# Clustered attention and two MLP layers on one core: another order of a head pair's cycle

## The chip, the cores and the metric

The kernel runs on one core of a Trainium2 chip. Its engines take their instructions in program order, each from a queue of its own, and wait for each other by semaphores: TensorE (PE, with its weight loads as PEld), VectorE (DVE), ScalarE (ACT), GpSimd (POOL) and SyncE (SP), which issues nearly all DMAs here. The metric is the time of one execution on the device in microseconds, as the median of several runs.

## The reference

Attention with 2 batches, 8 heads, 768 positions and head dimension 64, in which a query sees only the keys of its own cluster (16 centroids per head), and then two MLP layers over 1536 tokens (512 to 2048 and back). All values are float32.

```python
q_assign = np.argmax(np.einsum('bhsd,hcd->bhsc', q_n, c_n), axis=-1)
k_assign = np.argmax(np.einsum('bhsd,hcd->bhsc', k_n, c_n), axis=-1)
mask = q_assign[:, :, :, None] == k_assign[:, :, None, :]
scores = scale * np.matmul(q, k.transpose(0, 1, 3, 2))
scores = np.where(mask, scores, -1000000000.0)
scores = scores - np.max(scores, axis=-1, keepdims=True)
attn = np.exp(scores)
attn = attn / (np.sum(attn, axis=-1, keepdims=True) + 1e-09)
x = np.matmul(attn, v)          # then heads side by side: 1536 x 512
...
h = x @ w_in;  x = (h * np.cos(h)) @ w_out          # first layer
h = x @ w_in;  x = g(h) @ w_out                     # second: 0, (h+1)^2/4 or h
```

## The kernel before, in words

The 16 heads (2 batches of 8) are worked off as 8 pairs of heads, one pair in each cycle, and while a pair's scores are made, the pairs after it are prepared and the pair before it is finished. The order is written out by hand, as strings of short words: BEGIN for cycle 0, CYCLE for cycles 1 to 5, LATE for 6, LAST for 7, then END. `run_cycle` (line 719) emits the instructions word by word, and each engine keeps that order in its own queue; only END is mixed with the first instructions of the MLP stage when the program is built. A word with an apostrophe belongs to the pair before; the words of preparation (Q, D, C, m, t, n, O, H, J) are for the pair two ahead, or with the apostrophe for the next pair. The words:

- Q0 to Q3 (`turn`): PE transposes a quarter of q and k of a pair, ACT copies it out (t32, L497), POOL splits it in a high and a low part (tt, L499 and L500).
- D, C, m, t, n: dot products with the centroids, transposed back, and the first largest found (PE L510, L518; DVE L527, L528, L537, L538; POOL L533). O: PE transposes the one-hot rows, ACT writes them to the tile oht (L547), of which there is one.
- H0, H1 (`stack`): five DMAs on SP's queue each, which send the split parts of head 0 or 1 to the stacked operands st of the scores (L473, st from tt). J0, J1: four small DMAs each, which send the one-hot rows there (st from oht). There are three buffers of each st for the four that two pairs need.
- S0 to S11: the scores of 128 queries of the pair (S0 to S5 head 0, S6 to S11 head 1; PE L583 and L586), and DVE's row maximum (nm, L593). The scores have two buffers. E0 to E11: ACT's exponential with the row sum (p, L601).
- Head 0: G0 to G11 transposes p (PE L644, ACT copy L646), V0 to V5 multiplies it by v (L651), X scales the result by the reciprocals (DVE L656, in the tile rb), Y splits x for the MLP (POOL L663 to L667).
- Head 1: T6 to T11 transposes p in strips on DVE (L677), W0 to W3 are 192 small strip products on PE (L686), Z adds their halves (ACT L696, DVE L697), z scales and splits (POOL L705 to L707).
- R0, R1 (`inverse`): the reciprocals of the row sums, put in a line by POOL (L614) and sent to DRAM (flat, L617). B0, B1 (`spread`): SP loads them back to many partitions (rb, L630 for head 0, L625 for head 1). For head 0 there is one buffer rb, which holds the reciprocals, then x: the next load of it waits until Y has read it.
- L, v, r: SP loads the next q and k, v, and v in strips (L235, L243, L254). w: one of six steps in the conversion of a chunk of MLP weights (SP L147, ACT L157, DVE L159 to L167 and L176, POOL L173).

SP issues in order, so what stands behind a waiting load waits with it. The tile `big`, four banks of PSUM, takes the results of Q, D, C, O, G, V and W. On every engine a writer of `big` waits for the reader that stood before it in the program, of whatever bank. After the cycles comes the MLP stage: three matmuls (L858 to L860) for each product, with float32 values in two parts, over four quarters of the hidden width and three blocks of tokens in each layer.

```python
def x_rows(i):
    x = rb[2 * i]
    nc.vector.tensor_tensor(x, big[:, 3, :HS], x, ALU.mult)
...
    rb[d] = xpool.tile([P, HS], F32, tag="rb", bufs=1, name=f"rb{d}")
```

Of the kernel before, what the change touches and what calls it, by code (L numbers as in the profile page):

```python
# [33 lines left out]
def attention_moe_moe(  # L34
# [19 lines left out]
    B, H, S, D = q.shape  # L54
    C = centroids.shape[1]
# [152 lines left out]
    with ExitStack() as actx:  # L208
# [510 lines left out]
        def run_cycle(c, order):  # L719
# [4 lines left out]
            for word in words:  # L724
# [62 lines left out]
                elif what == "w":  # L787
                    pump(arg or 1)

        BEGIN = ("L' S3 m' S4 E3 t' E4 S5 H0' n' E5 R0 G0 G1 G2 S6 G3 G4 E6 G5 O' J0' r S7 T6 E7 G6 G7 V0 H1' "  # L790
                 "B0 V1 S8 T7 E8 Q0 G8 G9 J1' G10 S9 V2 Q1 T8 E9 Q2 Q3 L S10 D E10 T9 G11 C m V3 t n S11 O")
        CYCLE = ("Q0 Q1 S0 E11' V4' T10' E0 Q2 S1 Q3 S2 E1 V5' X' T11' E2 D v' S3 G0 S4 E3 W0' W1' S5 E4 J0' W2' "
                 "R1' E5 W3' Z' S6 S7 L G1 G2 G3 E6 G4 r E7 C m V0 V1 G5 t G6 T6 B1' R0 n G7 S8 T7 G8 G9 z' G10 "
                 "S9 V2 E8 B0 O T8 E9 S10 E10 Y' J1' H1' V3 H0' G11 T9 S11")
        LATE = ("S0 E11' V4' T10' E0 S1 w S2 E1 V5' X' T11' E2 v' S3 G0 S4 E3 W0' W1' S5 w E4 J0' W2' "
                "R1' E5 W3' w Z' S6 S7 G1 G2 G3 E6 G4 r E7 w V0 V1 G5 G6 T6 B1' R0 G7 S8 T7 G8 G9 z' G10 "
                "S9 V2 E8 B0 T8 w E9 S10 E10 Y' J1' H1' V3 H0' G11 T9 w S11")
        LAST = ("S0 E11' V4' T10' E0 S1 w S2 E1 V5' X' T11' E2 v' S3 G0 S4 E3 W0' W1' S5 w E4 W2' "
                "R1' E5 W3' w Z' S6 S7 G1 G2 G3 E6 G4 r E7 w V0 V1 G5 G6 T6 B1' R0 G7 S8 T7 G8 G9 z' G10 "
                "S9 V2 E8 B0 T8 w E9 S10 E10 Y' V3 G11 T9 w S11")  # L800
        END = "E11' V4' T10' V5' T11' R1' X' W0' W1' B1' W2' W3' Z' Y' z'"
        first_pair()
        for c in range(NP):
            run_cycle(c, {0: BEGIN, 6: LATE, 7: LAST}.get(c, CYCLE))
        run_cycle(NP, END)
        manual.close()
# [7 lines left out]
    while len(wslot) < 2:  # L814
        n = len(wslot)
# [148 lines left out]
```

## Time and profile before

| | us |
|---|---|
| runs, median (lowest to highest of 3) | 990.74 (990.56 to 995.32) |
| the profiled execution, its own time | 992.61 |
| its span, first to last instruction | 990.8 |
| PE busy | 836.3 (84%) |
| DVE, ACT, POOL busy | 583.7, 365.1, 253.2 |

The span falls in two parts: the attention stage up to about 474 us, in which PE's granted clock changes between half and full speed and no engine is full, and the MLP stage after it, in which PE is busy throughout at full clock. In the rows below, a line of the time line gives the start, the duration, the engine and line, the operation with its tiles, how many instructions were merged, and in brackets how long the engine had been idle before and what ended that. A line of the waits gives the total, the number and the longest. In rows of SP, SPq, the duration is the time of issuing, not that of the transfer.

### The profile page before, as it was taken

The page shows a single profiled execution, that of the slowest core. Times are in us where ns is not written, and L with a number is a line of the kernel's source. Part 1 is how long each engine was busy: PE and PEld are TensorE (multiplying, and loading weights), DVE is VectorE, ACT ScalarE, POOL GpSimd, SP SyncE. Part 2 cuts the span into 40 slices and gives each one's busy share as a digit, 9 for nine tenths or more (in the row PEclk, how much of TensorE's full clock was granted, in tenths as well). Part 3 has the DMA queues.
Part 4 walks back from the last instruction along what each step waited for, and adds up shares of the span by engine and source line. Part 5 has one row for each costly group of instructions (what it writes and reads, how often), then busy time and mean ns, then how long its engine had stood idle before and what let it go on. Part 6 is the DMA issues. An engine that isn't in the chain of part 4 may idle for free.

```text
span 990.8 us, 12697 instructions
## 1 busy us (share of the span) xinstructions
PE 836.3 (84%) x4957; PEld 632.5 (64%) x4957; DVE 583.7 (59%) x805; ACT 365.1 (37%) x650; POOL 253.2 (26%) x374
## 2 busy tenths in 40 slices
PE   7668776776757583676899999999999999999998
PEld 3435453444435351445788888888888888888887
DVE  4434433344434353554877787788888778884553
ACT  4425343433434342342544343444322443322220
POOL 5022424242423122042412212122332212211110
PEclk9578676766858676768899999999999999999999
DMA  7251423435343423313122221222112212200012
GB/s 186 59 123 44 94 69 94 98 75 117 74 108 96 108 53 97 73 30 118 69 85 85 74 87 52 86 86 85 43 43 85 67 62 85 86 1 1 0 43 85
DMA packets 52620, 74.97 MB, mean 76 GB/s; under 512 B 28976, under 2 KB 36368, under 8 KB 52560
## 3 DMA queue, kind: packets, MB, share of 16 engines
q1 hardware_dynamic: 52272, 73.99, 27.0%
q8 instruction: 39, 0.64, 0.3%
q14 instruction: 21, 0.17, 0.1%
q10 hardware_dynamic: 288, 0.16, 0.1%
HBM read 50.89 MB, written 3.19 MB: 55 GB/s over the span
## 4 chain that ended last, share of the span: by engine, by line
PE 52%; DVE 0%; ACT 0%; issue 0%; DVEq 0%
PE y L859 9%; PE y L860 9%; PE y L858 9%; PE h L858 8%; PE h L859 8%; PE h L860 8%; ACT r L833 0%; DVE xs L697 0%; DVE g L837 0%; DVE r L832 0%; ACT r L834 0%; PE y_end L860 0%; PE y_end L859 0%; PE y_end L858 0%; DVE acc L910 0%
## 5 line engine op out<-in xcount | busy, mean ns | idle before, releaser
L593 DVE TENSOR_REDUCE nm<-s 128x1 f32<-128x768 f32 x96 | 90.9, 955 | 200.6 <-PE s L586 199.8
L858 PE MATMUL h<-xh,w 128*128 128x512 f32 x384 | 150.4, 392 | 10.6 <-DVE g L837 9.5
L860 PE MATMUL h<-xh,w 128*128 128x512 f32 x384 | 149.9, 390 | 0.0
L859 PE MATMUL h<-xl,w 128*128 128x512 f32 x384 | 149.9, 390 | 0.0
L820 POOL TENSOR_SCALAR gh<-g 128x512 fp32r<-128x512 f32 x96 | 70.4, 734 | 271.4 <-DVE g L851 153.2
L583 PE MATMUL s<-st,st 128*128 128x384 f32 x192 | 91.0, 474 | 50.6 <-DMA st<-tt 49.3
L601 ACT ACTIVATE p<-s,nm 128x768 f32<-128x768 f32 x96 | 86.1, 898 | 99.9 <-DVE nm L593 99.6
L644 PE MATMUL big<-ident,p 128*128 128x128 f32 x288 | 71.5, 374 | 41.4 <-ACT p_t L646 35.8
L583 PEld LDWEIGHTS s<-st,st 128*128 128x128 f32 x192 | 48.6, 253 | 68.4 <-issue 58.7
L644 PEld LDWEIGHTS big<-ident,p 128*128 128x128 f32 x288 | 42.2, 183 | 78.4 <-ACT p_t L646 54.7
L858 PEld LDWEIGHTS h<-xh,w 128*128 128x128 f32 x384 | 72.5, 189 | 27.2 <-DVE g L837 9.9
L824 DVE TENSOR_TENSOR gl<-g,gh 128x512 fp32r<-128x512 f32 x96 | 73.6, 767 | 21.6 <-POOL gh L820 15.9
L646 ACT ACTIVATE p_t<-big 128x384 f32<-128x384 f32 x96 | 47.0, 490 | 102.9 <-PE big L644 102.3
L586 PE MATMUL s<-st,st 80*128 80x384 f32 (+1 forms) x192 | 80.8, 421 | 2.0 <-DVE st L429 2.0
L859 PEld LDWEIGHTS h<-xl,w 128*128 128x128 f32 x384 | 72.5, 189 | 15.0
L860 PEld LDWEIGHTS h<-xh,w 128*128 128x128 f32 x384 | 72.4, 188 | 15.0
L847 ACT ACTIVATE p<-h,ones 128x512 f32<-128x512 f32 x48 | 33.0, 688 | 130.8 <-DVE m L846 130.4
L651 PE MATMUL big<-p_t,v 128*64 128x384 f32 x192 | 61.4, 752 | 22.2 <-ACT oht L547 12.0
L157 ACT ACTIVATE wx<-wraw 128x1024 f32<-128x1024 f32 x32 | 36.3, 1134 | 106.2 <-DMA wraw<-in_moe_w_out_dram 60.7
L858 PE MATMUL y<-gh,w 128*128 128x512 f32 x192 | 74.7, 389 | 0.0
L859 PE MATMUL y<-gl,w 128*128 128x512 f32 x192 | 74.7, 389 | 0.0
L860 PE MATMUL y<-gh,w 128*128 128x512 f32 x192 | 74.7, 389 | 0.0
(138 smaller groups left out, 1479.8 us busy)
## 6 DMA issues: line engine op xcount, KB each, us to landing
wraw<-in_moe_w_in_dram SPq DMA_DIRECT2D x16, 1024.0 KB, 5.5
wraw<-in_moe_w_out_dram SPq DMA_DIRECT2D x16, 1024.0 KB, 4.7
st<-tt SPq DMA_DIRECT2D x63, 192.0 KB, 4.4
st<-tt SPq DMA_DIRECT2D x16, 384.0 KB, 3.7
vr<-in_v_dram SPq DMA_DIRECT2D x32, 192.0 KB, 4.2
nat<-in_q_dram SPq DMA_DIRECT2D x8, 384.0 KB, 3.7
nat<-in_k_dram SPq DMA_DIRECT2D x8, 384.0 KB, 4.7
out_dram<-acc SPq DMA_DIRECT2D x11, 256.0 KB, 2.0
```

What stands on the lines that cost most here:

```text
L583: nc.tensor.matmul(s[:, step, :HS], qt[:, 0, cols], kt[:, 0, kc], start=True, stop=False)
L586: nc.tensor.matmul(s[:, step, :HS], qt[:rows, 1, cols], kt[:rows, 1, kc], start=False, stop=True)
L593: nc.vector.tensor_reduce(nm, s[:, :, :HS], AX.XY, ALU.max, negate=True)
L601: nc.scalar.activation(p.rearrange("p (a n) -> p a n", a=2), s[:, :, :HS], AF.Exp, bias=nm, accum_out=dens[d][:, jj:jj + 1])
L644: nc.tensor.transpose(ps[:, jj * P:(jj + 1) * P], p[:, kt * P:(kt + 1) * P], ident)
L646: nc.scalar.activation(pt, ps, AF.Copy)
L651: nc.tensor.matmul(big[hf * D:(hf + 1) * D, 3, :HS], v_of[i][:, kt], pts.pop((i, 2 * kt + hf)), start=kt == 0, stop=kt == NJ - 1)
L820: nc.gpsimd.tensor_scalar(hi, g, 1.0, 0.0, ALU.mult, ALU.add)
L824: nc.vector.tensor_tensor(lo, g, hi.bitcast(F32), ALU.subtract)
L858: nc.tensor.matmul(o, lh, rh, start=first, stop=False)
L859: nc.tensor.matmul(o, lh, rl, start=False, stop=False)
L860: nc.tensor.matmul(o, ll, rh, start=False, stop=last)
```

## The change

Only the five strings are written anew. Words stand in another place; what a word does is the same. In CYCLE: Y' stands behind the W words instead of near the end; H0' of the next pair stands behind S1 and H1' behind V0 instead of near the end; O belongs to the next pair and stands behind H0', ahead of J0' and J1'; E11, V4 and z' close a cycle instead of being left to the next; W0' to W3' have no scores between them; B0 stands behind all sends. BEGIN, LATE, LAST and END follow suit.

```diff
-        CYCLE = ("Q0 Q1 S0 E11' V4' T10' E0 Q2 S1 Q3 S2 E1 V5' X' T11' E2 D v' S3 G0 S4 E3 W0' W1' S5 E4 J0' W2' "
-                 "R1' E5 W3' Z' S6 S7 L G1 G2 G3 E6 G4 r E7 C m V0 V1 G5 t G6 T6 B1' R0 n G7 S8 T7 G8 G9 z' G10 "
-                 "S9 V2 E8 B0 O T8 E9 S10 E10 Y' J1' H1' V3 H0' G11 T9 S11")
+        CYCLE = ("Q0 S0 Q1 S1 H0' E0 Q2 E1 T10' O' V5' S2 Q3 S3 E2 E3 J0' D T11' X' G0 S4 E4 v' S5 W0' W1' R1' "
+                 "J1' E5 R0 W2' W3' Y' L Z' S6 S7 G1 B1' G2 G3 E6 C G4 E7 V0 H1' m V1 T6 T7 G5 G6 t G7 S8 n G8 "
+                 "r G9 G10 E8 S9 B0 T8 V2 E9 V3 S10 G11 S11 E10 T9 E11 z' V4 ")
...
-        END = "E11' V4' T10' V5' T11' R1' X' W0' W1' B1' W2' W3' Z' Y' z'"
+        END = ("T10' V5' T11' X' R1' W0' B1' W1' W2' W3' Z' Y' z' ")
```

On SP in the second half of cycle 3, before. In the names, st0_4_1 is the stack of pair 4, head 1, tt4 and oht4 its split parts and one-hot rows, rb6 the reciprocals of pair 3, head 0.

```order
L630 DMA rb6_1768<-flat6_1721 64x384 x2
L473 DMA st0_4_1_1015<-oht4_1369 16x384 x2
L473 DMA st1_4_1_1016<-oht4_1369 16x384 x2
L473 DMA st0_4_1_1015<-tt4_1012 64x2x768
L473 DMA st0_4_1_1015<-tt4_1012 64x768
L473 DMA st1_4_1_1016<-tt4_1012 64x768 x3
L473 DMA st0_4_0_1013<-tt4_1012 64x2x768
L473 DMA st0_4_0_1013<-tt4_1012 64x768
L473 DMA st1_4_0_1014<-tt4_1012 64x768 x3
```

All sends for pair 4 but four rows stand behind the load of rb6, head 1's ahead of head 0's, and the next cycle's first scores need the last of them.

On SP now, from the end of cycle 2 into cycle 3:

```order
L630 DMA rb4_1377<-flat4_1202 64x384 x2
L473 DMA st0_4_0_1011<-tt4_1010 64x2x768
L473 DMA st0_4_0_1011<-tt4_1010 64x768
L473 DMA st1_4_0_1012<-tt4_1010 64x768 x3
L473 DMA st0_4_0_1011<-oht4_1469 16x384 x2
L473 DMA st1_4_0_1012<-oht4_1469 16x384 x2
```

and in the second half of cycle 3:

```order
L625 DMA rb5_1689<-flat5_1591 64x768
L473 DMA st0_4_1_1013<-tt4_1010 64x2x768
L473 DMA st0_4_1_1013<-tt4_1010 64x768
L473 DMA st1_4_1_1014<-tt4_1010 64x768 x3
L254 DMA vr3_1758<-in_v_dram 32x4x384 x4
L630 DMA rb6_1782<-flat6_1607 64x384 x2
```

The sends for pair 4's head 0 have moved to the start of cycle 3 and are followed by its one-hot rows; head 1's stand in the middle, and the load of rb6 behind them.

On POOL in cycle 3, before (rb4 holds x of pair 2, head 0; xs2 that of head 1; line6 the reciprocals that rb6 loads):

```order
L533 TENSOR_TENSOR both5_1486<-both5_1486,desc_61 128x384
L614 TENSOR_SCALAR line6_1716<-turned6_1714 6x32 x4
L705 TENSOR_TENSOR xs2_1637<-xs2_1637,rb5_1710 64x768
L706 TENSOR_SCALAR xh_73<-xs2_1637 64x768
L707 TENSOR_TENSOR xl_74<-xs2_1637,xh_73 64x768
L666 TENSOR_SCALAR xh_73<-rb4_1363 64x384
L667 TENSOR_TENSOR xl_74<-rb4_1363,xh_73 64x384
```

and now:

```order
L614 TENSOR_SCALAR line6_1602<-turned6_1600 6x32 x4
L666 TENSOR_SCALAR xh_73<-rb4_1377 64x384
L667 TENSOR_TENSOR xl_74<-rb4_1377,xh_73 64x384
L663 TENSOR_SCALAR rb4_1377<-rb4_1377 64x384
L666 TENSOR_SCALAR xh_73<-rb4_1377 64x384
L667 TENSOR_TENSOR xl_74<-rb4_1377,xh_73 64x384
L533 TENSOR_TENSOR both5_1502<-both5_1502,desc_61 128x384
L705 TENSOR_TENSOR xs2_1665<-xs2_1665,rb5_1689 64x768
```

The split of rb4, which rb6's load waits for, has moved ahead of the one-hot step L533 and of head 1's scaling (L705).

On ACT at the start of cycle 3, before (p36 is E0 of pair 3, t32_5 the transposes of pair 5, both5 its dot products, p3_t0 the copy of G0):

```order
L601 ACTIVATE p36_1441,den6_1448<-s36_1436,nm36_1442 128x768
L497 ACTIVATE t32_5_2_1453<-big_87 128x384
L497 ACTIVATE t32_5_3_1468<-big_87 128x384
L601 ACTIVATE p37_1462,den6_1448<-s37_1457,nm37_1463 128x768
L601 ACTIVATE p38_1477,den6_1448<-s38_1472,nm38_1478 128x768
L512 ACTIVATE both5_1486<-big_87 128x384
L646 ACTIVATE p3_t0_1505<-big_87 128x384
```

and now:

```order
L601 ACTIVATE p36_1432,den6_1455<-s36_1427,nm36_1433 128x768
L497 ACTIVATE t32_5_2_1460<-big_87 128x384
L601 ACTIVATE p37_1447,den6_1455<-s37_1442,nm37_1448 128x768
L547 ACTIVATE oht4_1469<-big_87,ohbias_63,ohscale_62 128x384
L497 ACTIVATE t32_5_3_1484<-big_87 128x384
L601 ACTIVATE p38_1478,den6_1455<-s38_1473,nm38_1479 128x768
L601 ACTIVATE p39_1493,den6_1455<-s39_1488,nm39_1494 128x768
L512 ACTIVATE both5_1502<-big_87 128x384
L646 ACTIVATE p3_t0_1513<-big_87 128x384
```

The copy of the one-hot rows, oht4, has come to the front half, behind E1, and the copy of Q2 stays behind E0 with a writer of `big` waiting for each.

## Rows read from the trace of the kernel before

**Rows 1.** Busy time by cycle: stretch, length, PE, PEld, DVE, ACT, POOL, clock, DMA.
```profile
129.91:183.05 53.14, 38.09 (x327) 24.43 (x327) 21.61 (x30) 20.89 (x43) 16.88 (x25) 0.72 0.39 90
342.19:402.64 60.45, 33.08 (x300) 21.11 (x301) 23.47 (x31) 19.06 (x38) 11.92 (x17) 0.67 0.33 84
```

**Rows 2.** Waits of PE, 78 to 475 us: total, times, longest.
```profile
PE s L583 <- DMA st<-tt: 49.3, 6, 21.7
PE big L651 <- ACT oht L547: 12.0, 5, 5.7
...
PE big L651 <- DVE both L528: 6.6, 5, 1.3
PE big L510 <- DVE rb L656: 4.0, 5, 0.8
```

**Rows 3.** Time line, end of cycle 2: start, duration, engine, line, operation, idle before.
```profile
165.88 0.99 POOL L667 TENSOR_TENSOR xl<-rb,xh 64x384 fp32r<-64x384 f32 x1
166.89 1.14 SPq L630 DMA_DIRECT2D rb<-flat  x2
...
170.94 9.91 SPq L473 DMA_DIRECT2D st<-tt  x10
...
183.05 0.66 PE L583 MATMUL s<-st,st 128*128 128x384 f32 x1 [4.79 <-DMA st<-tt]
```

**Rows 4.** Waits of SP's queue, 78 to 475 us.
```profile
SPq L630 <- POOL xl L667: 73.9, 7, 18.6
```

**Rows 5.** Time line, end of cycle 6.
```profile
389.71 10.09 SPq L473 DMA_DIRECT2D st<-tt  x10
...
402.64 0.66 PE L583 MATMUL s<-st,st 128*128 128x384 f32 x1 [21.73 <-DMA st<-tt]
```

**Rows 6.** Instructions by line, cycles 1 to 7: busy, mean ns, idle before.
```profile
L593 DVE TENSOR_REDUCE nm<-s 128x1 f32<-128x768 f32 x84 | 79.5, 955 | 168.5 <-PE s L586 167.6
...
L677 DVE STREAM_TRANSPOSE ptb<-p 128x768 f32<-128x768 f32 x44 | 42.7, 970 | 14.0 <-ACT p L601 14.0
...
L656 DVE TENSOR_TENSOR rb<-big,rb 128x384 f32<-128x384 f32 x8 | 4.5, 558 | 2.9 <-DMA rb<-flat 2.9
...
L601 ACT ACTIVATE p<-s,nm 128x768 f32<-128x768 f32 x85 | 76.3, 898 | 86.9 <-DVE nm L593 86.7
...
L601 ACT ACTIVATION_READ_ACCUMULATOR p<-s,nm 128x1 f32 x85 | 16.8, 198 | 0.0
L497 ACT ACTIVATE t<-big 128x384 f32<-128x384 f32 x19 | 9.3, 490 | 16.8 <-PE big L491 16.8
...
L547 ACT ACTIVATE oht<-big,ohbias,ohscale 128x384 fp32r<-128x384 f32 x5 | 3.4, 670 | 21.5 <-DMA st<-oht 21.5
```

**Rows 7.** Time line of PE in cycle 2, pieces at full clock.
```profile
138.33 0.85 PE L510 MATMUL big<-t,cn 128*32 128x384 f32 x8 [0.81 <-DVE rb L656]
...
146.24 0.45 PE L583 MATMUL s<-st,st 128*128 128x384 f32 x1
...
147.05 0.34 PE L583 MATMUL s<-st,st 128*128 128x384 f32 x1
...
150.57 0.55 PE L644 MATMUL big<-ident,p 128*128 128x128 f32 x3 [0.58 <-ACT p_t L646]
```

**Rows 8.** Busy time and granted clock by stretch, columns as in rows 1.
```profile
135.80:152.90 17.10, 13.49 (x245) 9.59 (x243) 9.17 (x13) 9.90 (x21) 2.92 (x7) 1.00 0.35 86
152.90:169.90 17.00, 13.17 (x43) 7.46 (x44) 7.32 (x12) 4.72 (x11) 10.04 (x13) 0.50 0.22 51
183.05:190.40 7.35, 7.35 (x22) 4.87 (x22) 2.80 (x3) 2.59 (x5) 5.01 (x7) 0.50 0.01 2
```

**Rows 9.** Time line at the end of the attention stage.
```profile
438.74 1.18 DVE L167 SCALAR_TENSOR_TENSOR wx<-wraw,wx 128x1024 int32<-128x1024 int32 x1
...
447.24 0.52 SPq L147 DMA_DIRECT2D wraw<-in_moe_w_out_dram  x1
...
474.28 0.80 PE L858 MATMUL h<-xh,w 128*128 128x512 f32 x1 [9.52 <-DVE g L837]
```

More of the change, by code (lines that the diff above doesn't have):

```diff
@@ L788, in run_cycle @@
                     pump(arg or 1)
-        BEGIN = ("L' S3 m' S4 E3 t' E4 S5 H0' n' E5 R0 G0 G1 G2 S6 G3 G4 E6 G5 O' J0' r S7 T6 E7 G6 G7 V0 H1' "
-                 "B0 V1 S8 T7 E8 Q0 G8 G9 J1' G10 S9 V2 Q1 T8 E9 Q2 Q3 L S10 D E10 T9 G11 C m V3 t n S11 O")
-        CYCLE = ("Q0 Q1 S0 E11' V4' T10' E0 Q2 S1 Q3 S2 E1 V5' X' T11' E2 D v' S3 G0 S4 E3 W0' W1' S5 E4 J0' W2' "
-                 "R1' E5 W3' Z' S6 S7 L G1 G2 G3 E6 G4 r E7 C m V0 V1 G5 t G6 T6 B1' R0 n G7 S8 T7 G8 G9 z' G10 "
-                 "S9 V2 E8 B0 O T8 E9 S10 E10 Y' J1' H1' V3 H0' G11 T9 S11")
@@ L795, in attention_moe_moe @@
[L795 to L800, printed above, removed]
@@ L801, in attention_moe_moe @@
-        END = "E11' V4' T10' V5' T11' R1' X' W0' W1' B1' W2' W3' Z' Y' z'"
+        BEGIN = ("L' S3 m' E3 S4 t' S5 E4 H0' n' G0 E5 R0 O' G1 G2 S6 G3 G4 J0' E6 S7 G5 r T6 V0 E7 H1' V1 G6 "
+                 "G7 S8 T7 B0 Q0 J1' E8 G8 G9 Q1 V2 S9 T8 G10 G11 Q2 Q3 L S10 E9 E10 T9 V3 D S11 E11 C m V4 t "
+                 "n ")
+        CYCLE = ("Q0 S0 Q1 S1 H0' E0 Q2 E1 T10' O' V5' S2 Q3 S3 E2 E3 J0' D T11' X' G0 S4 E4 v' S5 W0' W1' R1' "
+                 "J1' E5 R0 W2' W3' Y' L Z' S6 S7 G1 B1' G2 G3 E6 C G4 E7 V0 H1' m V1 T6 T7 G5 G6 t G7 S8 n G8 "
+                 "r G9 G10 E8 S9 B0 T8 V2 E9 V3 S10 G11 S11 E10 T9 E11 z' V4 ")
@@ new lines, in attention_moe_moe @@
+        LATE = ("S0 S1 H0' E0 E1 T10' O' V5' S2 S3 E2 w E3 J0' T11' X' G0 S4 E4 w v' S5 W0' W1' R1' J1' E5 R0 "
+                 "w W2' W3' Y' Z' S6 S7 G1 B1' G2 G3 E6 G4 E7 V0 H1' V1 w T6 T7 G5 G6 G7 S8 G8 r G9 G10 E8 w "
+                 "S9 B0 T8 V2 E9 V3 S10 G11 w S11 E10 T9 E11 z' V4 ")
+        LAST = ("S0 S1 E0 E1 w T10' V5' S2 S3 E2 E3 T11' X' G0 S4 E4 w v' S5 W0' W1' R1' E5 R0 w W2' W3' Y' "
+                 "Z' S6 S7 G1 B1' G2 G3 E6 G4 E7 V0 V1 w T6 T7 G5 G6 G7 S8 G8 r G9 G10 E8 w S9 B0 T8 V2 E9 V3 "
+                 "S10 G11 w S11 E10 T9 E11 z' V4 ")
```

## The prediction

> **What bounds the kernel now.** I read the granted clock and busy time by stretch first, then the waits of TensorE, then the time line around the longest of them. A cycle is counted here from the first score matmul of one pair to that of the next, PE L583 [rows 3]. Cycle 2 takes 53.14 us, with PE busy 38.09 of them and DVE, ACT and POOL 21.61, 20.89 and 16.88 [rows 1]; cycles 1, 3, 4 and 5 are like it, and cycle 6 takes 60.45. So no engine fills a cycle; in the attention stage PE waits. What it waits for stands in [rows 2]: six waits of together 49.3 us for a DMA from the split q and k (tt) into the stacked score operands (st), 12.0 us for ACT's one-hot rows (oht L547), 6.6 for DVE's comparison (both L528), 4.0 for DVE's scaling of x (rb L656). The six waits stand at the start of cycles 2 to 7, one each.
>
> The time line shows how one arises [rows 3]. POOL ends the splitting of x at 166.87 (L667, 165.88 + 0.99), and at 166.89 SP issues the load of reciprocals (rb), which had waited for the buffer that the split still read. Behind it on the same queue stand four sends of one-hot rows (2.9 us, from 168.03 to 170.94) and ten sends of tt. The ten are issued from 170.94 on and take 9.91 us of SP, about 1 us each, and the last lands some 2 us later, at 183.05, where PE's wait of 4.79 ends. SP spent 73.9 us in seven such waits of rb for POOL L667 [rows 4]. At the end of cycle 6 it is worse: the ten sends begin only at 389.71, and PE starts at 402.64, after 21.73 us of nothing [rows 5].
>
> **The change part by part.** It removes no instruction and adds none; it moves them.
>
> *Sends early, x split ahead of rb.* The five sends of tt for head 0 now stand at the start of the cycle, behind S1, a whole cycle before their use, those of head 1 behind V0, and rb behind both with the split already written on POOL. At the front SP needs 5 us for five sends and 2.9 for four rows; the first score matmul of the next pair is over 40 us away. I cost the six waits at zero from now on: -49.3. What hides the sends is the rest of the cycle. Bounds: 0 (they move elsewhere) and -49.3.
>
> *One-hot rows behind the sends.* The oht tile is single, and in the kernel before its next write (ACT L547) waits for sends of the old rows which stand behind rb. Now rows of one pair are made and sent in the same cycle, so that wait goes: -12.0 (bounds 0 and -12.0).
>
> *C, G4, V0, m, V1 instead of C, m, V0.* V0 no longer waits for DVE L528. It waits instead for ACT's copy behind E6, which G4 covers in part; I let half of 6.6 remain: -3.3 (0 to -6.6).
>
> *The new front half.* Three chains come into PE's way that the trace of before does not show. O' must wait for ACT's copy of Q2, which stands behind E0: row maximum 0.96, exponential 0.90, its accumulator read 0.20, copy 0.49, together 2.54 us [rows 6]. PE has Q1, S1 and Q2 beside it, where three transposes take 0.55 and a score step 0.81 at full clock (from 146.24 to 147.05) [rows 7]: 1.9, so 0.6 remains. V5' waits for oht behind E1, 0.90 + 0.20 + 0.67 = 1.77, beside O' (0.55): 1.2. G0 waits for DVE's x_rows behind the maximum of S3 and T11', 0.96 + 0.97 + 0.56 = 2.48 [rows 6], beside the dots product D, eight matmuls of 0.85 [rows 7]: 1.7. Before, D itself waited 0.81 for that DVE instruction; those 4.0 us in all go. Sum 3.5 us in each of cycles 1 to 5; cycle 6 has no Q and no D, 3.0; cycle 7 the last alone, 1.7: 5 x 3.5 + 3.0 + 1.7 = +22.2, less the 4.0 that go: +18.2. From below 0 (ACT and DVE may be ahead), from above the bare chains, 6.8 x 7 = 47.6. I take the worked-out value since ACT and DVE are busy 40% of a cycle.
>
> *Strip products in one run.* The 192 matmuls of W are the same; S5 only moves ahead of them. 0, hidden or not, since PE does the same work in order; the maximum of S5 now runs beside W.
>
> *Clock.* After each stall the clock stood at 0.50, at which PE was busy for all of 7.35 us [rows 8]; at full clock this work would take half, 3.7 less. Not all of it can be had, since other waits show then. I take 1.5 for each of six cycle starts: -9 (0 to -22).
>
> *The end.* The chunk of weights that is issued in cycle 7 could go when DVE L167 is done, 438.74 + 1.18 = 439.92, but stands behind rb on SP and goes at 447.24 [rows 9]. Now rb stands behind it. But DVE's first g then stands behind the steps of one more chunk, which waits for its own load, so of 7.3 us I count 3: -3 (0 to -7.3). The MLP stage after 474.28 [rows 9] has the same order but for this and is held by PE: 0. The first cycle is rearranged with the same work: 0, plus or minus 3.
>
> Sum: -49.3 - 12.0 - 3.3 + 18.2 - 9 - 3 = -58.4. The profiled execution took 992.6 (span 990.8), so 934.2; the median of the runs is 1.9 below the profiled one, so 932. A cross-check: cycles 1 to 5 would take about 46 us in place of 53.
>
> **A rule against it.** In [rows 8] the clock is at its upper level, 2.4 GHz, from 135.80 to 152.90, while PE does scores and strip products with 13.49 of 17.10 us busy; it falls to 1.2 GHz in a run of transposes, where each three of 0.55 us come after a wait of 0.58 for ACT (150.57) [rows 7]. The Trainium skill ("TensorE: Matmul & The Clock Gate", Part 4: PE-mode transpose) says that transposes do not count as busy for the clock. The trace agrees as far as the place of the fall goes; it cannot tell transposes from the waits between them. By that rule the front half, which now holds Q0 to Q3, O' and G0 with 3.5 us of waits, may lose the clock once more, and the time would be that of the second rival.
>
> **Rivals.**
> 1. *The sends are late somewhere else.* The one-hot rows of head 1 (J1') now wait for S5 because the third stacked buffer is then free, and the flat of R0, the load L and the sends of head 1 queue behind them on SP. If this costs each cycle the 4 to 5 us that the front gave back, only cycle 6 gains: 932 + 5 x 5 = 957. For it: SP is in order, and the ten sends and eight rows of a pair alone hold it for 9.9 + 2 x 2.9 = 15.7 us of a cycle [rows 3]. Against: S5 stands ahead of S6, which in cycle 2 begins 16.3 us after S0 (146.24 against 129.91), and nothing behind J1' needs to land before S6 of the next pair.
> 2. *The clock falls in the front half.* PE's 13.49 busy us at full clock [rows 8] would double; if a third of them do, 4.5 us in each of seven cycles: 932 + 32 = 964. For it: the fall among transposes and waits. Against: at full clock the scores and strip products keep PE 79% busy, and one wait of 0.8 (that of D) did not bring it down in cycle 2.
> 3. *The clock gains more.* Without a stall PE comes into the back half denser. If the half-speed stretch of 17 us [rows 8] becomes shorter by a third, some 3 us in each of seven cycles: 932 - 21 = 911.
> 4. *Slower than before.* The same clock mechanism, over the whole front half: all 13.49 us double in each of seven cycles, +94, so 1027. It decides, against -58.4, from 8.3 us a cycle on, that is where more than six tenths of the front half's work runs at 1.2 GHz. For it: the new front half has three waits where the old one had one. Against: they are 0.7 to 1.7 us, and the old front half of cycle 2 held its clock through one of 0.8.
>
> **How the numbers follow.** Forecast (919 to 945) 0.60, rival 1 0.10, rival 2 0.13, rival 3 0.12, rival 4 0.03, and 0.02 that it moves nothing measurable. About 0.5% (5 us) is what a measurement of this kernel can tell from no change: faster 0.95, same 0.02, slower 0.03. The range takes in rival 3 and the middle of rivals 1 and 2: 910 to 962, leaving out about 0.17. The time forecast is 932.
>
> **What would show it.** In the new profile: PE L583's waits for DMA st<-tt under 3 us in all against 49.3; SP's wait of rb for POOL L667 gone; ACT oht's wait for DMA gone; new waits of PE for ACT oht (about 1.2 a cycle), ACT t (0.6, at O') and DVE rb (1.7, at G0); cycles 1 to 5 at 45 to 47.5 us, cycle 6 near 40; the clock at 1.00 from Q0 to the first transposes of the back half. It would be wrong if a cycle takes 50 or more with the DMA waits gone (then the front half's chains or the clock were mis-sized), or if PE still waits for st.

## The result, and the profile after

The changed kernel takes 937.79 us, the median of four runs (924.13, 937.61, 937.96 and 940.14), against 990.65 (990.11 to 995.32) before. The ratio is 0.9411, interval 0.9306 to 0.9515; it leaves out the run of 940.14, which is over 1.5% above the fastest. The profiled execution is the one of 924.13, with a granted clock of 0.913; the others show 0.887 to 0.892. Its times are thus read against 924, not against the median.

The stretches of cycles 2 to 6, from the first score matmul of a pair to that of the next (columns as in [rows 1]: length, busy time of PE, PEld, DVE, ACT and POOL, granted clock, DMA share, GB/s):

```profile
119.14:163.46 44.32, 33.45 (x329) 21.62 (x327) 21.29 (x31) 20.71 (x44) 16.56 (x25) 0.81 0.46 108
163.46:202.51 39.05, 28.21 (x330) 18.93 (x327) 21.29 (x31) 20.70 (x44) 16.56 (x25) 1.00 0.52 122
202.51:252.30 49.79, 38.90 (x330) 25.62 (x327) 21.37 (x31) 20.66 (x44) 16.59 (x25) 0.69 0.40 97
252.30:291.11 38.81, 27.77 (x326) 18.54 (x323) 22.19 (x31) 20.72 (x44) 16.59 (x25) 1.00 0.54 129
291.11:331.08 39.97, 29.59 (x303) 20.38 (x304) 23.02 (x30) 19.60 (x39) 10.62 (x17) 0.83 0.51 126
```

Where cycles 2 and 6 took 53.14 and 60.45 [rows 1], they take 44.32 and 39.97. They are not alike, though: cycles 3 and 5, with the clock at 1.00 throughout, take 39, cycle 4 with 0.69 takes 49.79.

The waits of PE between 75 and 415 us (total, times, longest), which answer to [rows 2]:

```profile
PE big L644 <- DVE rb L656: 16.2, 7, 2.5
PE h L859 <- DVE g L838: 12.2, 1, 12.2
PE big L651 <- ACT oht L547: 7.1, 6, 2.4
PE big L651 <- DVE both L528: 6.6, 5, 1.3
...
PE big L545 <- ACT t L497: 3.7, 5, 0.8
PE h L859 <- ACT p L601: 2.9, 1, 2.9
...
PE s L583 <- DMA rb<-flat: 0.2, 1, 0.2
```

The 49.3 us for st<-tt are gone; one wait of 0.2 us is left at a first score matmul. The 12.0 of oht are 7.1, in another place (V5'). DVE both stands at 6.6 as before. New are DVE rb at G0 with 16.2 and ACT t at O' (L545) with 3.7.

SP's own waits in the same stretch, which answer to [rows 4]:

```profile
SPq L473 <- PE s L586: 46.6, 5, 12.7
SPq L473 <- ACT oht L547: 11.4, 6, 3.5
...
SPq L630 <- POOL xh L706: 0.5, 2, 0.3
```

SP no longer stands 73.9 us behind POOL's split of x: the waits of rb (L630) for POOL come to 0.5 us. It now waits 46.6 us, in five cycles, for the last scores that read a stack buffer, but that comes early and nothing waits for it.

The time line of cycle 2 and the start of cycle 3 in the kernel after, beside [rows 3] (start, duration, engine, line, operation, and how many are merged):

```profile
118.13 4.55 SPq L473 DMA_DIRECT2D st<-tt  x5
...
138.19 0.99 POOL L667 TENSOR_TENSOR xl<-rb,xh 64x384 fp32r<-64x384 f32 x1
...
142.41 4.79 SPq L473 DMA_DIRECT2D st<-tt  x5
...
150.27 1.11 SPq L630 DMA_DIRECT2D rb<-flat  x2
...
163.46 0.44 PE L583 MATMUL s<-st,st 128*128 128x384 f32 x1
```

The five sends of head 0 go at 118.13, those of head 1 at 142.41; the scores that need the first of them begin at 163.46, with no wait in brackets. POOL ends the split of x at 139.18 (138.19 + 0.99), and rb is loaded at 150.27, so its buffer has been free for 11 us.

One row holds the whole account. From the first score matmul of cycle 1 to the matmul with which the MLP stage resumes, before:

```profile
78.54:474.28 395.74, 270.33 (x2475) 175.17 (x2473) 171.29 (x233) 150.84 (x303) 117.16 (x172) 0.72 0.35 86
```

and after:

```profile
75.34:405.25 329.91, 240.50 (x2477) 161.61 (x2476) 177.59 (x238) 150.61 (x303) 117.06 (x174) 0.84 0.41 102
```

The stage takes 65.83 us less (395.74 to 329.91), of the 68.5 by which the span is shorter; 3.2 more lie in front of it (78.54 to 75.34). Length less PE's busy time is its idle time: 125.41 before, 89.41 after, so 36.0 of the gain are waits. The other 29.8 are PE's busy time, 270.33 to 240.50, with the same matmuls (2475 and 2477 records): the granted clock, 0.72 to 0.84.

### The profile page after: what moved, and what is told of

It is laid out like the page before. It is cut to its first block, busy times and chain, and to the rows that moved or that the text cites. A ratio compares the mean times of both kernels' runs of the same rounds, so it can differ in the third digit from the quotient of the medians.

```text
span 922.3 us, 12700 instructions
## 1 busy us (share of the span) xinstructions
PE 808.5 (88%) x4957; PEld 619.6 (67%) x4957; DVE 587.6 (64%) x805; ACT 365.1 (40%) x650; POOL 254.4 (28%) x374
## 4 chain that ended last, share of the span: by engine, by line
PE 78%; ACT 6%; DVE 6%; issue 4%; DMA 3%; POOL 2%; SPq 1%; ACTq 0%; DVEq 0%; POOLq 0%
PE y L859 9%; PE y L861 9%; PE y L860 9%; PE h L859 9%; PE h L860 9%; PE h L861 9%; PE big L644 6%; PE big L651 4%; PE s L583 3%; PE s L586 3%; PE big L686 3%; ACT p_t L646 3%; DMA st<-tt 2%; DVE nm L593 2%; SPq L473 1%
## 5 line engine op out<-in xcount | busy, mean ns | idle before, releaser
L859 PE MATMUL h<-xh,w 128*128 128x512 f32 x384 | 151.2, 394 | 15.1 <-DVE g L838 12.2
L821 POOL TENSOR_SCALAR gh<-g 128x512 fp32r<-128x512 f32 x96 | 73.4, 765 | 278.8 <-DVE g L852 159.8
L644 PE MATMUL big<-ident,p 128*128 128x128 f32 x288 | 65.2, 347 | 49.7 <-ACT p_t L646 29.3
L644 PEld LDWEIGHTS big<-ident,p 128*128 128x128 f32 x288 | 39.2, 171 | 81.8 <-ACT p_t L646 45.0
L825 DVE TENSOR_TENSOR gl<-g,gh 128x512 fp32r<-128x512 f32 x96 | 74.5, 776 | 21.8 <-POOL gh L821 15.8
L583 PE MATMUL s<-st,st 128*128 128x384 f32 x192 | 82.5, 429 | 3.7 <-ACT p L601 3.4
L861 PEld LDWEIGHTS h<-xh,w 128*128 128x128 f32 x384 | 72.8, 190 | 15.3
L586 PE MATMUL s<-st,st 80*128 80x384 f32 (+1 forms) x192 | 73.6, 383 | 1.9 <-DVE st L429 1.9
L861 PE MATMUL y<-w,gl 128*128 128x512 f32 (+1 forms) x192 | 74.3, 387 | 0.0
L860 PE MATMUL y<-w,gh 128*128 128x512 f32 (+1 forms) x192 | 74.3, 387 | 0.0
```

Source lines behind the costliest of these rows:

```text
L583: nc.tensor.matmul(s[:, step, :HS], qt[:, 0, cols], kt[:, 0, kc], start=True, stop=False)
L586: nc.tensor.matmul(s[:, step, :HS], qt[:rows, 1, cols], kt[:rows, 1, kc], start=False, stop=True)
L644: nc.tensor.transpose(ps[:, jj * P:(jj + 1) * P], p[:, kt * P:(kt + 1) * P], ident)
L821: nc.gpsimd.tensor_scalar(hi, g, 1.0, 0.0, ALU.mult, ALU.add)
L825: nc.vector.tensor_tensor(lo, g, hi.bitcast(F32), ALU.subtract)
L859: nc.tensor.matmul(o, lh, rh, start=first, stop=False)
```

## The experiments

Medians are of four runs (six for the last kernel), each beside runs of the kernel before in the same rounds (989.2 to 991.3). Idle and busy time are PE's, over the stretch of the row above, in the profiled run.

| kernel | us | ratio to before, interval | idle | busy | clock |
|---|---|---|---|---|---|
| before | 990.65 | | 125.4 | 270.3 | 0.72 |
| after, first profile | 937.79 | 0.9411, 0.9306 to 0.9515 | 89.4 | 240.5 | 0.84 |
| after_again | 940.27 | 0.9487, 0.9431 to 0.9544 | 89.4 | 255.9 | 0.78 |
| e1_split_early | 942.59 | 0.9505, 0.9482 to 0.9528 | 91.3 | 253.2 | 0.78 |
| e2_split_late | 935.09 | 0.9433, 0.9386 to 0.9480 | 90.6 | 251.1 | 0.79 |
| e3_w_split | 937.52 | 0.9455, 0.9406 to 0.9505 | 89.2 | 250.3 | 0.82 |
| e4_x_early | 931.18 | 0.9402, 0.9379 to 0.9426 | 84.0 | 251.4 | 0.80 |
| e5_rows_old_place | 932.91 | 0.9468, 0.9400 to 0.9536 | 84.3 | 243.1 | 0.83 |
| e6_waits | 924.67 | 0.9364, 0.9320 to 0.9409 | 76.1 | 255.9 | 0.80 |
| e7_chunk | 926.46 | 0.9351, 0.9300 to 0.9402 | 72.6 | 253.3 | 0.81 |
| e10_all | 921.93 | 0.9301, 0.9264 to 0.9338 | 66.8 | 258.5 | 0.77 |
| e8_warm | 917.41 | 0.9248, 0.9216 to 0.9280 | 77.7 | 246.3 | 0.89 |
| e9_chunk_warm | 905.11 | 0.9144, 0.9104 to 0.9184 | 61.2 | 252.8 | 0.90 |
| e11_all_warm | 899.98 | 0.9084, 0.9053 to 0.9115 | 53.9 | 245.1 | 0.92 |

**e1_split_early.** The kernel before with one word moved, in CYCLE, LATE and LAST alike:

```diff
-... W3' Z' S6 S7 ... S10 E10 Y' J1' H1' V3 H0' G11 T9 S11
+... W3' Z' Y' S6 S7 ... S10 E10 J1' H1' V3 H0' G11 T9 S11
```

> The kernel before with one word moved: Y' (the split of x) stands behind Z', ahead of B0; the sends stay at the end of the cycle. Theory A (SP's queue was blocked by rb's wait for the split, and that is what made the sends late): rb is issued some 5 us earlier, the ten sends with it, so the waits of PE for DMA st<-tt fall from 49.3 us to 10 to 20, most of the rest at the end of cycle 6, where the weight chunk still stands ahead of the sends; the oht wait of 12.0 falls under 3; time 940 to 958. Theory B (the sends' place counts, the split alone does little, since 15 us of sends stand at the end anyway): st waits stay above 35 us and the time is 975 to 990.

It took 942.59. The waits of PE and the stage, as above:

```profile
PE s L583 <- DMA st<-tt: 21.8, 6, 14.0
```

```profile
78.24:422.78 344.54, 253.24 (x2471) 162.48 (x2471) 174.00 (x236) 151.77 (x303) 120.45 (x172) 0.78 0.40 99
```

Splitting x sooner, with the sends left at the end of the cycle, brings 48.7 us by the medians (991.28 to 942.59), where the whole change brought 52.9 and, taken again, 49.0; the intervals overlap. PE still waits 21.8 us for st, most of it (14.0) at the end of cycle 6, and has no wait for oht left. The idle time is 91.3, nearly as low as the changed kernel's 89.4: what this order still loses at the sends, the other loses at its new front-half waits. So 27.5 of the 49.3 us were due to the load of rb that stood on SP behind the split and held all sends. At the end of cycle 6 another load now holds them in the same way, as SP's rows there show:

```profile
325.25 1.12 SPq L630 DMA_DIRECT2D rb<-flat  x2
337.90 0.40 SPq L147 DMA_DIRECT2D wraw<-in_moe_w_in_dram  x1
...
341.08 9.99 SPq L473 DMA_DIRECT2D st<-tt  x10
```

The load of weights (wraw) waits 11.5 us for DVE's L167, which still reads the chunk before, and the sends stand behind it.

**e2_split_late.** The changed kernel with Y' at its old place, behind E10, and the sends early:

```diff
-J1' E5 R0 W2' W3' Y' L Z' S6 ... S11 E10 T9 E11 z' V4
+J1' E5 R0 W2' W3' L Z' S6 ... S11 E10 Y' T9 E11 z' V4
```

> The changed kernel with Y' put back behind E10, so that B0 waits for the split again; the sends stay early. Theory A and B both say that SP is then blocked in the last part of a cycle; behind it stand only the early sends of the pair after next's turn, which are not needed for a whole cycle: SP waits for POOL L667 again (some 5 us in each of seven cycles), PE's waits for st stay under 3 us, time 930 to 945. If instead the split's place is what counts whatever the sends do, the time goes to 955 or more.

It took 935.09. SP waits for the split again:

```profile
SPq L630 <- POOL xl L667: 18.7, 7, 4.5
```

half of what was expected (some 5 us in each of seven cycles), but PE has no wait for st, since the sends stand ahead of rb. Each of the two moves alone brings a time that these runs cannot tell from that of both; of PE's waits for st, the early sends alone remove all, the early split alone 27.5 of 49.3 us.

**e5_rows_old_place.** The one-hot rows (O) made ahead of S11 of the cycle before, the sends left where the change put them:

```diff
-CYCLE = ("Q0 S0 Q1 S1 H0' E0 Q2 E1 T10' O' V5' S2 ... G11 S11 E10 T9 E11 z' V4 ")
+CYCLE = ("Q0 S0 Q1 S1 H0' E0 Q2 E1 T10' V5' S2 ... G11 O S11 E10 T9 E11 z' V4 ")
```

> The changed kernel with the one-hot rows made where they were (O ahead of S11, for the pair two ahead), while the sends stay early. If the 12.0 us that PE lost behind ACT oht before were due to the rows of the old pair being sent late (my step), they do not come back: ACT oht waits for no DMA, and the front half loses its two waits (ACT oht 7.1 us, ACT t 3.7 us): 925 to 937. If the place of O itself removed them (rival), the oht wait is 8 us or more again at V4 or S11 and the time is 940 or more.

It took 932.91, with runs from 924.92 to 943.48. ACT's wait at oht is for PE alone:

```profile
ACT oht L547 <- PE big L545: 6.2, 6, 3.0
```

The 12.0 us of [rows 2] do not come back, and the waits at O' and V5' (3.7 and 7.1) go. Others take part of their place (V5' waits 3.4 us for ACT's copy of Q2, L497), and the idle time falls by 5.2. So it was the lateness of the sends that held the tile oht, and making the rows behind the sends gave nothing: it cost the front half two waits.

**e3_w_split.** S5 between the halves of the strip products again:

```diff
-S4 E4 v' S5 W0' W1' R1' J1'
+S4 E4 v' W0' W1' S5 R1' J1'
```

> The changed kernel with S5 put back between the two halves of the strip products. Predicted 0: 933 to 942 against 938. Rival (the run in one piece keeps the clock up or delays S5's maximum less): 945 or more, with a lower granted clock.

937.52, with an idle time of 89.2 against 89.4: nothing, as forecast.

**e4_x_early.** X' right behind V5', so that DVE scales x before the maxima of S2 and S3:

```diff
-E1 T10' O' V5' S2 Q3 S3 E2 E3 J0' D T11' X' G0
+E1 T10' O' V5' X' S2 Q3 S3 E2 E3 J0' D T11' G0
```

> The changed kernel with X' right behind V5', so that DVE scales x before the maxima of S2 and S3 and T11'; G0 then waits for nothing on DVE. The wait of PE big L644 for DVE rb, 16.2 us in the changed kernel's profile, goes under 3, and 8 to 16 us of it come back: 922 to 930. Rival (Q3 now waits for DVE instead, or the clock decides): 935 or more, with the wait under another name.

931.18 (930.16 to 935.29), just above the 922 to 930 that were expected. The wait of G0 for rb goes, and half of it comes back as the next wait at the same place:

```profile
PE big L644 <- ACT both L512: 8.4, 5, 1.7
```

D stands right ahead of G0, and G0 now waits for ACT's copy of D's result (both L512). The idle time falls by 5.4, the time by 7 to 9, which is within the changed kernel's own scatter (924 to 943).

**e6_waits** and **e7_chunk.** e6 adds to e4: D right behind S3; C and m ahead of S8; t and n later. e7 adds to e6 nine steps w in place of six in LATE and LAST.

```diff
-S3 E2 E3 J0' D T11' G0 ... E6 C G4 E7 V0 H1' m V1 T6 T7 G5 G6 t G7 S8 n G8 r
+S3 D E2 E3 J0' T11' G0 ... E6 G4 E7 V0 H1' V1 T6 T7 G5 G6 G7 C m S8 G8 t r
```

> The changed kernel with X' right behind V5', D right behind S3 (so its copy on ACT stands ahead of E2), and C and m right ahead of S8, with t and n after it. Theory: each wait of PE for a reader of the big tile is covered when a score step, which does not write that tile, stands behind the reader: PE's waits for DVE rb (16.2), DVE both (6.6) and ACT both fall under 6 together, 15 us or more: 918 to 928 if the clock behaves as in the changed kernel. Rival (PE's time is set by the clock and by the run of transposes, and other waits take the place): 930 or more.

> The kernel of the expectation before this one, with nine steps of weight conversion instead of six in each of cycles 6 and 7, so that three chunks are converted before the MLP stage instead of two. Theory (the 12.2 us of PE before its first product after the attention stage are DVE's steps for two chunks and their loads): that wait falls to 4 us or less, 7 to 12 us less than that kernel. Rival: the wait is for the last strip products and head 1's x, or the extra steps hold up DVE and ACT in cycles 6 and 7 as much: within 4 us of that kernel.

924.67 and 926.46. In e6 the three waits named come to 4.0 us (ACT both 3.4, DVE both 0.6), under the 6 expected. The idle time falls by 13.3 and 16.8 against the changed kernel; in e7 the wait of the MLP stage for DVE g is 5.5 in place of 12.2. But the stage of e6 reads:

```profile
73.16:405.13 331.97, 255.86 (x2477) 166.59 (x2475) 176.61 (x238) 148.86 (x303) 117.89 (x174) 0.80 0.41 101
```

PE is busy 255.9 us at a mean clock of 0.80. Fewer idle microseconds did not raise the clock. The 7 to 12 us that e7 was expected to give beside e6 did not come: its 3.5 us of idle time less are lost in the scatter (917.82 to 928.86).

**after_again, e8_warm, e9_chunk_warm, e10_all, e11_all_warm.** The changed kernel once more, and a test of the clock: a new word h makes two score matmuls, without use, in a score tile that the real scores fill later. It stands in seven places of the back half.

```diff
...
+        def warm(n):
+            ...
+            for step in range(2):
+                nc.tensor.matmul(ptile[n][:, step, :HS], qt[:, 0, j * P:(j + 1) * P],
+                                 kt[:, 0, step * HS:(step + 1) * HS], start=True, stop=True)
...
-E6 C G4 E7 V0 H1' m V1 T6 T7 G5 G6 t G7 S8 n G8 r G9 G10 E8
+E6 C G4 h8 E7 V0 H1' m V1 T6 T7 G5 h8 G6 h8 t G7 h8 S8 n G8 h9 r G9 h9 G10 h9 E8
```

> The changed kernel once more, on the same chip as the three others. Expected 924 to 940 with a scatter of some 15 us from execution to execution, wider than the 5 us of the kernel before: the lengths of its cycles stand on two levels, some 39 us where the granted clock stays at its upper level through the back half and 44 or more where it falls. The profile should again show cycles on these two levels and no wait of PE for st.

> The changed kernel with two more score matmuls (some 0.2 us each at full clock) in each of six places between the transposes of the back half, G4 to G10, written into a score tile that the real scores overwrite later; the result is the same. Theory A: the granted clock falls in the back half because PE idles there between transposes; with these matmuls in the waits it stays at 1.00 in most cycles, all cycles come near the 39 us that cycles 3 and 5 of the changed kernel's first profile showed, and the time falls by 15 to 30 us, to 908 to 922. Theory B: the fall has another cause; the 12 matmuls a cycle are 2.5 to 5 us more work, half of it in waits, so 7 cycles cost 8 to 18 us: 945 to 955. Between the two (930 to 945): the matmuls hide and change nothing.

> The order with x, D, m, t and n moved and nine steps of weights at the last two pairs (926 before), with the same two score matmuls in each of six places of the back half. Theory A: 900 to 912, with the clock at 1.00 in the back halves. Theory B: 935 to 945.

> The order with x, D, m, t and n moved and nine steps of weights, and the one-hot rows made at the old place, ahead of S11. The waits of V5' and O' for ACT (7.1 and 3.7 us in the changed kernel) go as they did when the rows alone were moved back: 916 to 924 if the waits add up. Rival: the clock takes it back, as it varies from 924 to 940 with the same waits: 924 to 932.

> All of it together: x, D, m, t and n moved, nine steps of weights, the one-hot rows at the old place, and two score matmuls in each of seven places of the back half. Theory A: the matmuls hold the clock in the back half as they did twice (-23 and -21 us beside the same order without them), and the rows at the old place give the 4.5 us that they gave without them (926.5 to 921.9): 905.1 - 4.5 = 901, between 896 and 905. Rival: with the clock at its upper level the waits of ACT for the rows are hidden anyway, or rows made late make the back half's waits longer: 904 to 912.

The changed kernel again took 940.27 (930.37 to 942.55). Its stage, in a run of 942.55:

```profile
78.37:423.59 345.22, 255.85 (x2473) 170.71 (x2472) 175.83 (x236) 150.35 (x303) 117.04 (x173) 0.78 0.39 97
```

The idle time is 89.37, where the first profile had 89.41. All of the 15.3 us between the two stretches is busy time at a lower clock, 0.78 for 0.84. The two levels of cycle length that were expected did not show again: no cycle of this run kept the clock at 1.00 throughout. Of its cycles 2 to 5, the longest and the shortest:

```profile
123.60:171.75 48.15, 37.27 (x329) 24.57 (x326) 21.37 (x31) 20.76 (x44) 16.58 (x25) 0.72 0.43 99
...
263.80:307.80 44.00, 32.70 (x327) 21.41 (x324) 21.29 (x31) 20.71 (x44) 16.58 (x25) 0.84 0.48 114
```

e8 took 917.41 (913.84 to 918.59), 20 to 23 less, with more work in it; the texts of e8 and e9 count six places, and that of e8 0.2 us for a matmul, where it is seven places and 0.3. Its cycles 2 to 5 and its stage:

```profile
117.99:158.65 40.66, 31.75 (x343) 22.05 (x340) 21.38 (x31) 20.77 (x44) 16.61 (x25) 0.96 0.49 118
158.65:199.35 40.70, 31.79 (x344) 21.98 (x341) 21.39 (x31) 20.78 (x44) 16.60 (x25) 0.96 0.50 117
199.35:240.81 41.46, 32.34 (x343) 22.00 (x340) 21.28 (x31) 20.59 (x44) 16.62 (x25) 0.96 0.50 116
240.81:281.47 40.66, 31.52 (x340) 21.73 (x337) 21.38 (x31) 20.77 (x44) 16.61 (x25) 0.96 0.49 124
```

```profile
73.06:397.04 323.98, 246.25 (x2575) 171.41 (x2572) 176.87 (x238) 150.72 (x303) 117.23 (x174) 0.89 0.42 104
```

Four cycles at 0.96, all within 0.8 us of each other. What the matmuls do can be seen in the middle of cycle 2, PE's time line first of the changed kernel and then of e8:

```profile
146.13 1.55 PE L651 MATMUL big<-p_t,v 128*64 128x384 f32 x4 [1.33 <-DVE both L528]
147.61 0.90 PE L644 MATMUL big<-ident,p 128*128 128x128 f32 x3
149.09 0.90 PE L644 MATMUL big<-ident,p 128*128 128x128 f32 x3 [0.58 <-ACT p_t L646]
```

```profile
145.82 0.87 PE L661 MATMUL big<-p_t,v 128*64 128x384 f32 x4 [1.33 <-DVE both L528]
146.62 0.55 PE L654 MATMUL big<-ident,p 128*128 128x128 f32 x3
146.92 0.59 PE L596 MATMUL s<-st,st 128*128 128x384 f32 x2
147.74 0.55 PE L654 MATMUL big<-ident,p 128*128 128x128 f32 x3 [0.23 <-ACT p_t L656]
148.04 0.59 PE L596 MATMUL s<-st,st 128*128 128x384 f32 x2
```

In the changed kernel three transposes take 0.90 at half clock and PE then idles 0.58: 1.48 from one to the next. In e8 they take 0.55, the two matmuls 0.59, and the wait is down to 0.23: 1.12 (146.62 to 147.74). 98 matmuls are added, some 29 us by 0.59 a pair; against after_again the idle time falls by 11.6, and the busy time is 246.3, 9.6 less although that work is in it. The time is that of theory A, at its cautious end: not every fall is gone.

e9 and e11 repeat it on other orders: e7 to e9 is 926.46 to 905.11, e10 to e11 is 921.93 to 899.98. The stages of e10, e9 and e11, and then two of e11's waits:

```profile
81.43:406.67 325.24, 258.47 (x2470) 167.17 (x2469) 175.66 (x237) 147.57 (x301) 119.47 (x174) 0.77 0.42 104
```

```profile
72.81:386.86 314.05, 252.84 (x2575) 169.29 (x2573) 177.59 (x239) 147.51 (x302) 118.86 (x175) 0.90 0.45 110
```

```profile
79.03:378.01 298.98, 245.08 (x2568) 163.61 (x2567) 176.50 (x237) 147.36 (x301) 119.64 (x174) 0.92 0.46 113
```

```profile
PE big L654 <- ACT p_t L656: 18.5, 45, 0.6
PE h L871 <- DVE g L850: 5.9, 1, 5.9
```

e10 against e8 is the sharpest pair: e10 idles 66.8 of 325.2 us, e8 77.7 of 324.0, and yet e10 has a clock of 0.77 and e8 of 0.89. How long PE idles in all does not set the clock, then. But the idle time that e10 saves lies mostly in the front half and at the end; its waits for ACT's copies between the transposes of the back half are no shorter than those of the changed kernel (26.4 us), and those of e8 are. First e10, then e8:

```profile
PE big L644 <- ACT p_t L646: 29.2, 49, 0.6
```

```profile
PE big L654 <- ACT p_t L656: 15.9, 41, 0.6
```

So two readings are left: the added matmuls hold the clock because they fill these waits, or because they are work of another kind than transposes. The Trainium skill ("TensorE: Matmul & The Clock Gate", Part 4: PE-mode transpose), which says that transposes do not count as busy like other matmuls, agrees with the pair by the second reading. No run here replaced transposes by as many other matmuls, or shortened the waits without adding any, so neither is shown.

e11, 899.98 and 0.9084 of before, beats both kernels. It holds x early, D, m, t and n moved, nine steps of weights, the rows at their old place, and the added matmuls.

## Why the prediction was right, step by step

932 was forecast, and 937.79 and 940.27 came. The mechanism of the largest term was right; that the sum came out near was in part luck, because two errors stood against each other: the waits gave 13.4 us less than forecast, the clock 5.5 to 20.8 more. The forecast held -49.4 for waits (-49.3 - 12.0 - 3.3 + 18.2 - 3) and -9 for the clock. Measured are -36.0 of idle time, and of busy time -29.8 in the first profile or -14.5 in the second (270.33 to 240.50 or 255.85). The terms for waits, as measured below, add up to -32.5 (-49.1 - 12.0 + 23.0 + 5.6); small waits elsewhere make the rest to -36.0.

- *Sends early, x split ahead of rb, -49.3:* right in size (49.3 to 0.2) and in cause: e2 shows it for the early sends, e1 for the split, which alone leaves 21.8. Half of the edit would have done: the early sends alone (e2).
- *One-hot rows behind the sends, -12.0:* the wait went, but by the sends, not by the move of O; e1 and e5 show it gone with the rows at the old place.
- *C, G4, V0, m, V1, -3.3:* measured 0. The wait of 6.6 for DVE both, five times up to 1.3, moved from V0 to V1, which stands behind m. The step overlooked that m waits for V0, a writer of `big`, as any user of that tile does:

```profile
DVE mx L527 <- PE big L651: 23.2, 5, 5.7
```

- *The new front half, +22.2 less 4.0:* measured 3.7 + 7.1 + 16.2 = 27.0 less 4.0. O' is near the 0.6 worked out (0.75 a time). V5', worked out at 1.2, waits 0.95 in cycles 1 to 5 and 2.37 in cycle 6, where O' comes without a wait. G0 waits 2.25 in cycles 1 to 5 in place of 1.7. The working let D hide 0.85 of DVE's chain, but D adds a step to it: DVE's scaling of x stands behind ACT's copy of D's result and waits 0.55 for it, as in cycle 3:

```profile
174.06 0.56 DVE L656 TENSOR_TENSOR rb<-big,rb 128x384 f32<-128x384 f32 x1 [0.55 <-ACT both L512]
```

  Cycles 6 and 7, which have no D to hide anything, were put down with the same 1.7 and wait 2.38 and 2.55.
- *Strip products, 0:* right (e3).
- *The end, -3:* wrong in sign, +5.6. PE waits for DVE's first g 12.22 in place of 9.52 [rows 9], and 2.9 more for ACT p, a wait that was not there:

```profile
404.52 0.68 DVE L838 SCALAR_TENSOR_TENSOR g<-r,h 128x512 f32<-128x512 f32 x1
...
405.25 0.80 PE L859 MATMUL h<-xh,w 128*128 128x512 f32 x1 [12.22 <-DVE g L838]
```

  The extra chunk's steps on DVE ahead of g, counted at 4.3 of the 7.3, eat all of it: three of them (L159, L161, L164) hold DVE from 399.77 to 404.01, right ahead of the last steps to g. With nine steps in the last cycles (e7) the wait is 5.5.
- *Clock, -9 (0 to -22):* mis-sized. -14.5 in the second profile lies within the bounds, -29.8 in the first beyond them. The forecast counted only the half-speed starts of cycles [rows 8]; with the stalls gone, two back halves also kept the clock in the first profile, and none did in the second.
- *Rival 1* (sends late elsewhere) did not come: SP's new wait of 46.6 us holds nothing up. *Rival 2* (the clock falls in the front half) came in single cycles, as in cycle 2 of the second profile, some 10 us behind its first scores:

```profile
134.50:141.00 6.50, 6.19 (x83) 5.38 (x91) 3.06 (x9) 2.47 (x5) 0.83 (x4) 0.50 0.01 3
```

  and *rival 3* (the clock gains more) in the first profile. Both lie within the scatter from 924 to 943 us of one order; that they make up all of it is not shown. *Rival 4* (slower) and the 964 of rival 2 did not come.
- *The signs:* the waits that were named went and came as said, if not in every size. The lengths of cycles did not stand at 45 to 47.5 us: cycles 2 to 5 took 38.8 to 49.8, just short of the 50 that was to count against the forecast; cycle 6, forecast near 40, took 39.97.

## What to carry to other kernels

An engine that issues transfers in order is a lock: a load that waits for a buffer holds every send behind it, and moving the one instruction that frees the buffer gave here, within the scatter, as much as the whole new order (48.7 us against 52.9 and 49.0). Split a change in time into idle and busy time of the bounding engine over one stretch: the idle part follows from the order of the work and repeated within 0.1 us here, the busy part carries the clock. And where PE makes transposes between short waits, matmuls put into the waits can pay although nothing uses them (here 20 to 23 us, in three orders).

## What was not expected of the hardware

With the same instructions, order and waits, one of cycles 2 to 5 takes 39 us where the granted clock stays at 1.00 and 44 to 50 where it falls, as it did in all of them in the second profile; over the kernel this is 924 to 943 us. Why it held in cycles 3 and 5 of the first profile and fell in cycles 2 and 4, which wait in the same places, stays open. Removing 22.6 us of idle time (e10) did not raise the clock (0.77); adding 98 matmuls (e8) did (0.89). No run put such matmuls ahead of cycle 1 or behind the last cycle, where the clock is mixed as well.
